# An S5 scan mixer with an MLP gate: even states in place of the direct matrix, row-half products, and a second product and outputs with features on partitions

## The chip, the core and the metric

The kernel runs on one core of a Trainium2 chip. The metric is device microseconds of one execution. The kernel before has a median of 153.38 us over three runs (153.37 to 153.44).

## What is computed

The input `x` has 2048 positions of 448 features, all tensors are bf16, and the weights are 448 by 448 or 448 by 1792 and back. Two branches read the normalised input, and their product is added to `x`.

```python
xn = layernorm(x)
# A: diagonal complex recurrence over the positions, 448 states
Bu = einsum("bld,pd->blp", xn, B_bar)
h  = Lam_bar * h + Bu[:, t, :]                  # t = 0 .. 2047
s  = 2 * einsum("blp,dp->bld", hseq, C).real + xn * Dskip
# B: MLP on a second layernorm
g  = silu(gelu(layernorm(xn) @ w1 + b1) @ w2 + b2)
out = x + s * g
```

## The kernel before

The 2048 positions are worked in four groups of 512. A group is two blocks of 256 positions, and on the chip 128 partitions hold a pair of neighbouring positions each, an even one and an odd one (`par` 0 and 1). The recurrence is run over pairs: one step of it takes the state over two positions, so a group has 256 steps (`NK`).

For each group the work is, by the names of the code:

- **Normalisation**: statistics on VectorE, scales on GpSimd or VectorE, two normalised copies (`xn_sb` for branch A, `xn2_sb` for B), each turned to features on partitions by transposing DMAs on SyncE's queue (`xnT`, `xn2T`).
- **First MLP product** (`mm1_run`, line 802): 14 blocks of 128 hidden features. The 448 input features are split into halves of 64 rows, so that two matmuls of 64 rows run beside each other on the two halves of TensorE's array. Blocks go in pairs through three pairs of PSUM banks; ScalarE's GELU (line 806) empties them into `gT`.
- **Second MLP product** (`mm2`, line 829): the 14 hidden blocks are the weights one by one, `w2` (448 columns) is what streams, and the result has positions on partitions. VectorE adds the bias (line 832). In groups 0 and 3 ScalarE then takes SiLU of it; in groups 1 and 2 it takes tanh, which needs no other function table than GELU's, and VectorE finishes the gate (line 837).
- **State inputs** (`bu`, line 730): `Bu` for a pair of positions needs 896 input features (an even and an odd position). Seven row blocks of states by seven chunks of 128 features give 49 matmuls of 256 columns a group. The matrix `BT` is `B` and `Lam*B` next to each other, formed in the kernel (`lb`, lines 659 to 662), and turned by transposing DMAs.
- **Recurrence** (`ssm`, lines 745 to 776): VectorE turns the inputs by a table of angles (`WT`), scans the decay (`TENSOR_TENSOR_SCAN`, line 754), ScalarE copies to bf16, VectorE turns back into `h_sb`. The tables come from ScalarE's Sin (line 641), which lies in SiLU's function table.
- **Outputs** (`ym`, lines 872 to 894): odd positions are `CQ` times the state; even positions are `CZ` times the state before, plus a direct matrix `M0` times the position's own input (line 875). `M0` is formed once by 28 matmuls (`m0`, lines 698 and 713). VectorE multiplies by the gate and adds `x`, SyncE stores.

TensorE starts with filler matmuls on constants (line 422).

Nothing of the order is decided on the chip. Every operation is a task, `ORDER` is a list of task numbers that sets the order of each engine, `SECOND` lists the tasks that run on the second of two permitted engines, and semaphore waits are put in from the tasks' reads and writes. Each engine takes its own instructions strictly in that order, so an instruction that waits holds up all behind it on that engine. The function tables of ScalarE are loaded by tasks as well; where a function is not in the table that is loaded, the build puts a load in.

## Time and profile before

| | |
|---|---|
| median of three runs | 153.38 us |
| profiled execution: span | 151.8 us |
| TensorE busy | 148.0 us, 98% |
| VectorE busy | 127.4 us, 84% |
| ScalarE busy | 99.0 us, 65% |
| GpSimd busy | 41.7 us, 27% |
| TensorE matmuls | 1135 |
| share of TensorE in the chain that ended last | 97% |

The profile's span runs from the first to the last instruction of one execution. The page gives no other time for that execution; the median of the timed runs is 1.6 us above the span, for what lies around it. The chain that ended last is followed back from the last instruction, at each step to what released it. It stands on TensorE nearly all the way, so what TensorE does, and when it waits, is the time.

### The profile page before, as it was taken

The page shows a single profiled execution, that of the slowest core. Times are in us where ns is not written, and L with a number is a line of the kernel's source. Part 1 is how long each engine was busy: PE and PEld are TensorE (multiplying, and loading weights), DVE is VectorE, ACT ScalarE, POOL GpSimd, SP SyncE. Part 2 cuts the span into 40 slices and gives each one's busy share as a digit, 9 for nine tenths or more (in the row PEclk, how much of TensorE's full clock was granted, in tenths as well). Part 3 has the DMA queues.
Part 4 walks back from the last instruction along what each step waited for, and adds up shares of the span by engine and source line. Part 5 has one row for each costly group of instructions (what it writes and reads, how often), then busy time and mean ns, then how long its engine had stood idle before and what let it go on. Part 6 is the DMA issues. An engine that isn't in the chain of part 4 may idle for free.

```text
span 151.8 us, 2990 instructions
## 1 busy us (share of the span) xinstructions
PE 148.0 (98%) x1135; PEld 87.9 (58%) x1135; DVE 127.4 (84%) x267; ACT 99.0 (65%) x183; POOL 41.7 (27%) x101
## 2 busy tenths in 40 slices
PE   7999999999999999999999999999999999999992
PEld 7986755454566577545444556764454666555551
DVE  2877979899969979999999996479968726999984
ACT  3797998878789549997898610463579834067410
POOL 5367872053020820010456006200072031000201
PEclk9999999999999999999999999999999999999999
DMA  4999999989896300700004032710331001100023
GB/s 113 251 308 393 274 235 147 180 157 131 150 271 175 68 0 0 138 0 4 0 0 63 4 60 41 158 60 5 60 97 26 4 0 52 69 0 0 4 78 103
DMA packets 31236, 14.73 MB, mean 97 GB/s; under 512 B 24752, under 2 KB 30774, under 8 KB 31222
## 3 DMA queue, kind: packets, MB, share of 16 engines
q1 hardware_dynamic: 30912, 14.26, 43.3%
q0 software_dynamic: 160, 0.23, 0.8%
q8 instruction: 9, 0.15, 0.4%
q14 instruction: 5, 0.04, 0.2%
q10 hardware_dynamic: 150, 0.05, 0.1%
HBM read 6.89 MB, written 1.84 MB: 57 GB/s over the span
## 4 chain that ended last, share of the span: by engine, by line
PE 97%; DVE 1%; issue 0%
PE psum L802 29%; PE psum L829 28%; PE psum L730 14%; PE psum L872 13%; PE psum L875 4%; PE psum L422 3%; PE psum L713 3%; PE psum L878 1%; PE psum L460 1%; PE psum L698 1%; DVE tmp L894 0%; DVE psum L888 0%; PE psum L603 0%; PE psum L530 0%; PE psum L531 0%
## 5 line engine op out<-in xcount | busy, mean ns | idle before, releaser
L802 PE MATMUL psum<-xn2T,w_sb 64*128 64x512 bf16 (+1 forms) x462 | 44.6, 345 | 0.1
L829 PE MATMUL psum<-w_sb,gT 128*128 128x448 bf16 x224 | 44.4, 353 | 0.0
L806 ACT ACTIVATE gT<-psum,b1f 128x512 bf16<-128x512 f32 (+1 forms) x66 | 36.0, 625 | 10.4 <-PE psum L802 10.2
L802 PEld LDWEIGHTS psum<-xn2T,w_sb 64*128 64x128 bf16 x462 | 23.9, 109 | 19.8 <-ACT gT L806 2.3
L829 PEld LDWEIGHTS psum<-w_sb,gT 128*128 128x128 bf16 x224 | 21.6, 98 | 20.3 <-issue 0.6
L417 ACT ACTIVATE u_sb<-psum 128x512 bf16<-128x512 f32 (+2 forms) x22 | 10.5, 478 | 23.0 <-PE psum L730 22.7
L730 PE MATMUL psum<-xnT,BT 128*128 128x256 bf16 x196 | 24.0, 273 | 0.0
L730 PEld LDWEIGHTS psum<-xnT,BT 128*128 128x128 bf16 x196 | 19.0, 98 | 5.4 <-issue 1.1
L894 POOL TENSOR_TENSOR tmp<-t,x_all 128x448 bf16<-128x448 bf16 x5 | 5.1, 1030 | 33.1 <-DVE t L891 30.7
L754 DVE TENSOR_TENSOR_SCAN s_w<-dk,vs 128x774 f32<-128x774 f32 x8 | 14.0, 1760 | 0.1
L501 ACT ACTIVATE xn_sb<-x_all,lnw 128x448 bf16<-128x448 bf16 (+2 forms) x21 | 13.0, 662 | 1.2 <-DVE xn_sb L500 1.1
L417 ACT ACTIVATE vs<-s_w 64x256 bf16<-64x256 f32 (+2 forms) x16 | 10.9, 681 | 2.6 <-DVE s_w L754 1.5
L872 PE MATMUL psum<-CZ,h_sb 128*128 128x448 bf16 x56 | 11.9, 353 | 0.0
L832 DVE TENSOR_TENSOR o<-psum,b2bc 128x448 f32<-128x448 f32 x16 | 9.8, 615 | 1.5 <-PE psum L829 1.3
L872 PE MATMUL psum<-CQ,h_sb 128*128 128x448 bf16 (+2 forms) x54 | 10.5, 332 | 0.0
L399 DVE BATCH_NORM_STATS2 lnst<-x_all 128x6 f32<-128x448 bf16 x12 | 7.0, 615 | 2.2 <-DMA x_all<-in_A_x_dram 2.2
L872 PEld LDWEIGHTS psum<-CZ,h_sb 128*128 128x128 bf16 x56 | 5.4, 98 | 4.7 <-DVE lnmv L405 0.4
L872 PEld LDWEIGHTS psum<-CQ,h_sb 128*128 128x128 bf16 x54 | 5.1, 98 | 4.0 <-DVE t L888 0.4
L875 PE MATMUL psum<-M,xnT 128*128 128x448 bf16 x32 | 7.4, 352 | 0.0
L886 DVE TENSOR_TENSOR Cr<-psum,xd 128x448 f32<-128x448 f32 x7 | 4.3, 621 | 3.5 <-PE psum L878 3.4
L481 POOL TENSOR_TENSOR lnw<-lnw,mhalf 128x8 f32<-128x8 f32 x3 | 7.1, 2367 | 0.2
L500 DVE TENSOR_SCALAR xn_sb<-x_all,lnw 128x448 bf16<-128x448 bf16 (+2 forms) x19 | 6.9, 397 | 0.0
(161 smaller groups left out, 191.3 us busy)
## 6 DMA issues: line engine op xcount, KB each, us to landing
out_dram<-tmp SPq DMA_DIRECT2D x7, 224.0 KB, 2.0
x_all<-in_A_x_dram SPq DMA_DIRECT2D x3, 448.0 KB, 4.2
w_sb<-in_B_w_dram SPq DMA_DIRECT2D x3, 448.0 KB, 8.5
w_sb<-in_B_w_dram SPq DMA_DIRECT2D x3, 384.0 KB, 4.8
vs<-in_A_C_re_dram SPq DMA_DIRECT2D x1, 392.0 KB, 11.3
Bn<-in_A_B_im_dram SPq DMA_DIRECT2D x1, 336.0 KB, 10.2
Bn<-in_A_B_re_dram SPq DMA_DIRECT2D x1, 336.0 KB, 10.6
vs<-in_A_C_im_dram SPq DMA_DIRECT2D x1, 336.0 KB, 11.1
```

The lines of the kernel that those rows point to most:

```text
L399: dve([lambda e, b=b, par=par, q=q: e.bn_stats(lnst[:, q, :], x_all[:, 2 * g + b, par, :])], [f"x{2 * g + b}"] , [f"st{q}"], 0.62, prio)
L417: kb.either(("act", [lambda e, o=o, i=i: e.activation(o, i, ACT.Copy) for o, i in pairs]), ("dve", [lambda e, o=o, i=i: e.tensor_copy(o, i ...
L481: power = fns + [lambda e: e.tensor_tensor(w(2), w(0), mhalf[:].to_broadcast([128, 2, nq]), ALU.pow), lambda e: e.tensor_tensor(w(3), mean ...
L501: ("act", [lambda e, o=o, i=i: e.activation(o, i, ACT.Identity, bias=nb, scale=rs) for o, i in parts], 0.75, 0.2)]
L730: fns = [lambda e, r=r, m=m, d=d: e.matmul(psum[:, 4, r * NK:(r + 1) * NK], BT[:, m, d, :], xnT[:, gx, d, :], start=(d == 0), stop=(d == 6 ...
L754: dve(lambda e, so=so, vi=vi: e.tensor_tensor_scan(so, dk[:].rearrange("p i c -> p (i c)"), vi, 0.0, ALU.mult, ALU.add), ["v", "vl", "dk", ...
L802: return lambda e: e.matmul(view(bk[k]), w1_sb[rows, d, fcol(2 * j + k)], rhs[rows, d, :, :], start=not second and n == 0, stop=second and ...
L806: act([lambda e, k=k: e.activation(gT[:, gb, 2 * j + k, :].rearrange("p (r c) -> p r c", r=2)[:, :, cols], view(bk[k]), ACT.Gelu_apprx_tan ...
L829: fns = [lambda e, fi=fi: e.matmul(psum[:, bk, 0:D], gT[:, gb, fi, q * 128:(q + 1) * 128], w2_sb[:, fi, :], start=(fi == 0), stop=(fi == N ...
L832: dve(lambda e: e.tensor_tensor(o2[:, fb, :], psum[:, bk, 0:D], b2bc[:], ALU.add), [f"ps{bk}", "b2bc"], [f"oo{fb}"], 0.62, prio - 76)
L872: fns = [lambda e, k=k: e.matmul(psum[:, bk, c0:c1], h_sb[:, hb, k, k0:k0 + 128], cm[:, k, c0:c1], start=(k == 0), stop=False) for k in ra ...
L875: fns += [lambda e, d=d: e.matmul(psum[:, bk, c0:c1], xnT[:, gx, d, xs], M0[:, d, c0:c1], start=False, stop=(d == 3)) for d in range(4)]
```

## The change

The kernel is rewritten in five respects. New names are those of the changed kernel.

1. **No direct matrix.** `M0` and its 28 matmuls go. The state inputs are now formed in two steps: first the part of the even positions (kept as `ue`), then the odd part is added in the same PSUM banks. VectorE adds `ue` to the turned state, and this even state `hz` gives the even outputs with `CQ`; the odd outputs take `CZ` times the state (`hx`).
2. **State inputs on row halves** (`bu_phase`): as in the first MLP product, 64 rows each, 98 matmuls of 256 columns a group, written as stages that stand between the phases of the next group's first MLP product. They take one of its three pairs of PSUM banks.
3. **Second MLP product with features on partitions** (`mm2`): `w2` is the weight, `gT` streams, 512 columns. Features 384 to 447 go as two column halves (64 columns wide, the two position parities beside each other). The bias is a column, so ScalarE takes **SiLU from PSUM** and VectorE's addition goes. SiLU is used in all four groups; ScalarE's table is switched to GELU and back in each.
4. **Outputs with features on partitions** (`yt`): 256 columns each, features 384 to 447 as column halves. The skip term is a VectorE operation from PSUM (groups 0 to 2) or a diagonal matrix `Dg` on TensorE (group 3). The product with the gate (`t3`) is turned back by transposing DMAs (`out_dma`, groups 0 to 2) or by TensorE (`out_pe`, group 3).
5. **The orders** `ORDER`, `SECOND` and `STEPS` are new. `mm2` and `yt` now take two PSUM banks in turn.

```diff
-                    fns = [lambda e, fi=fi: e.matmul(psum[:, bk, 0:D], gT[:, gb, fi, q * 128:(q + 1) * 128], w2_sb[:, fi, :],
-                                                     start=(fi == 0), stop=(fi == NF - 1)) for fi in range(a, z)]
...
-                dve(lambda e: e.tensor_tensor(o2[:, fb, :], psum[:, bk, 0:D], b2bc[:], ALU.add), [f"ps{bk}", "b2bc"], [f"oo{fb}"], 0.62, prio - 76)
...
+                        pe([lambda e, fi=fi: e.matmul(psum[:, bk, :], w2_sb[:, fi, 128 * j:128 * j + 128], gT[:, gb, fi, :], start=fi == 0, stop=fi == NF - 1)
+                            for fi in range(a, z)], rd, [f"ps{bk}"])
...
+                act(lambda e: e.activation(g_sb[:, gb, 512 * j:512 * j + n], psum[:, bk, 0:n], ACT.Silu, bias=b2c[:, j:j + 1]), [f"ps{bk}", "db", f"Ws{g}"], [f"g{gb}_{j}"])
...
+                            fns.append(lambda e, rows=rows, bank=bank, m=m, o=o, n=n: e.matmul(
+                                psum[:, bank, c * NK:(c + 1) * NK], BT[rows, m, 4 * o + n, :], xnT[rows, gx, 4 * o + n, :],
+                                start=not (odd or second or n or c), stop=bool(second and n == 3), skip_group_check=bool(odd or c)))
...
+                dve(lambda e: e.tensor_tensor(hz[:, hb, :, :], hx[:, hb, :, 0:NK], ue[:, hb, :, :], ALU.add),
...
+                    pe([lambda e, k=k: e.matmul(psum[:, bk, NK:512], CZ[:, k, cols], hx[:, hb, k, 1:NK + 1], start=k == 0, stop=k == 6) for k in range(7)], ko, [f"ps{bk}"])
+                    fns = [lambda e, k=k: e.matmul(psum[:, bk, 0:NK], CQ[:, k, cols], hz[:, hb, k, :], start=not by_pe and k == 0, stop=not by_pe and k == 6, skip_group_check=by_pe) for k in range(7)]
...
-                kb.add("act", lambda e: e.preload_act_table_set("gelu_apprx_tanh_and_others"), ["W"] * (g == 0) + [f"g{n % 8}" for n in range(4 * g, 4 * g + 4)] * (9 >> g & 1), [f"Wg{g + 1}"], sem=f"gelu{g + 1}")
...
+                    gelu_table(g, gate(g - 1))
```

The last pair of lines of the diff: the load of GELU's table for group 1 waited for the angle tables (`"W"`) as well as for the gate of group 0; now it waits for the gate alone.

How the instructions move is told at three places. The first is TensorE after the first MLP product of group 0. Before, with `gT,w_sb` the second MLP product (56 matmuls), `xn2T,w_sb` the first product of group 1 and `xnT,BT` the state inputs of group 0:

```order
L802 MATMUL psum<-xn2T,w_sb 128x2x128 x56
L829 MATMUL psum<-w_sb,gT 128x448 x56
L802 MATMUL psum<-xn2T,w_sb 128x512 x90
L730 MATMUL psum<-xnT,BT 128x256 x14
L802 MATMUL psum<-xn2T,w_sb 128x512 x8
```

After, with lines 785 and 788 the second MLP product, 663 the first and 692 the state inputs:

```order
L663 MATMUL psum<-xn2T,w_sb 128x2x128 x56
L785 MATMUL psum<-gT,w_sb 128x512 x42
L788 MATMUL psum<-gT,w_sb 64x256 x28
L692 MATMUL psum<-xnT,BT 128x256 x28
L663 MATMUL psum<-xn2T,w_sb 128x512 x28
L692 MATMUL psum<-xnT,BT 128x256 x12
L663 MATMUL psum<-xn2T,w_sb 128x512 x6
```

The state inputs moved from behind the first product of group 1 to its front and between its phases. The last row is the third pair of hidden blocks, which goes into the banks of the first pair and so needs the first two GELUs of group 1 done.

The second place is ScalarE between the gate of group 0 and the GELUs of group 1. Before (line 834 is SiLU, 641 Sin, 619 the load of GELU's table):

```order
L834 ACTIVATE g_sb<-o 128x448 x2
L641 ACTIVATE WT<-s_w,sgn 128x256
L834 ACTIVATE g_sb<-o 128x448
L619 ACT_TABLE_LOAD
L806 ACTIVATE gT<-psum,b1f 128x512 x12
```

After (line 791 is SiLU, 590 Sin, 451 and 457 the normalised input, 605 a product with a coefficient of `B`, 476 the load that the code asks for):

```order
L605 ACTIVATE tmp<-Bn,cw 128x512
L451 ACTIVATE xn_sb<-x_all,lnw 128x448
L590 ACTIVATE WT<-s_w 128x3x258
L590 ACTIVATE WT<-s_w,sgn 128x4x258
L457 ACTIVATE xn_sb<-xn_sb 128x2x64
L791 ACTIVATE g_sb<-psum,db 128x256
L791 ACTIVATE g_sb<-psum,db 128x512
L590 ACTIVATE WT<-s_w,sgn 128x258
L476 ACT_TABLE_LOAD
L590 ACT_TABLE_LOAD
L590 ACTIVATE WT<-s_w,sgn 128x258
L669 ACT_TABLE_LOAD
```

The last Sin now stands behind the load of GELU's table. It is not in that table, so the build puts a load ahead of it and another behind it.

The third place is the end of VectorE's list. Before (line 888 is the product with the gate, 894 the addition of `x`):

```order
L888 SCALAR_TENSOR_TENSOR t<-psum,g_sb 128x448
L888 SCALAR_TENSOR_TENSOR t<-psum,g_sb 128x256
L894 TENSOR_TENSOR tmp<-t,x_all 128x448
L888 SCALAR_TENSOR_TENSOR psum<-psum,g_sb 128x192
L894 TENSOR_TENSOR tmp<-psum,Cr 128x192
```

After (line 826 is the skip term, 828 the product with the gate, 770 the even states of group 3, 843 and 862 additions of `x`, 862 from TensorE's transposes):

```order
L770 TENSOR_TENSOR Bn<-hx,ue 128x1792
L826 SCALAR_TENSOR_TENSOR tmp<-xnT,db,psum 128x512
L828 TENSOR_TENSOR t<-tmp,g_sb 128x512 x2
L828 TENSOR_TENSOR t<-psum,g_sb 128x512
L862 TENSOR_TENSOR Bn<-psum,x_all 128x4x128
L828 TENSOR_TENSOR t<-psum,g_sb 128x512
L843 TENSOR_TENSOR Bn<-Cr,x_all 128x2x384
L828 TENSOR_TENSOR t<-psum,g_sb 128x512
L843 TENSOR_TENSOR Bn<-Cr,x_all 128x2x384
L862 TENSOR_TENSOR Bn<-psum,x_all 128x4x128 x2
L828 TENSOR_TENSOR t<-psum,g_sb 128x256
L862 TENSOR_TENSOR Bn<-psum,x_all 128x4x64
```

The state chain of group 3, the outputs of group 2 and those of group 3 now end on VectorE in one list, and behind the last product TensorE turns it back before the last addition.

More of the change, by code (lines that the diff above doesn't have):

```diff
@@ L11 @@
 F32 = dt.float32
-PINNED = -1e5
 ENGS = ("pe", "act", "dve", "pool", "sp")
@@ new lines, in one_mm @@
+                def one_mm(k, n, h):
+                    rows, d = slice(64 * h, 64 * h + 64), (0, 1, 2 + h, 3 - h)[n]
+                    return lambda e: e.matmul(view(bk[k]), w1_sb[rows, d, fcol(2 * j + k)], rhs[rows, d, :, :], start=not second and n == 0, stop=second and n == 3)
+                pe([one_mm(h if not second else 1 - h, n, h) for n in range(4 if second else 3) for h in (0, 1)],
+                   xk2 + [f"w1_{c}", f"w1r_{c}"] + ([f"w1c_{c}"] if second else []), [f"ps{bk[0]}", f"ps{bk[1]}"], split=True)
```

962 lines of the change are left out of this document (459 added, 503 removed), and 36 rows, old and new, of the table ORDER.

## The prediction

> **What bounds the kernel now.** I read the page first, then the chain that ended last, then ScalarE's and VectorE's timelines around the places where TensorE will newly have to wait.
>
> ```profile
> span 151.8 us, 2990 instructions
> PE 148.0 (98%) x1135; PEld 87.9 (58%) x1135; DVE 127.4 (84%) x267; ACT 99.0 (65%) x183; POOL 41.7 (27%) x101
> PE 97%; DVE 1%; issue 0%
> ```
>
> TensorE is busy from end to end and is the chain. Work taken off it is worth its full length, and any wait that the new order puts on it costs its full length, since it has no idle time left to absorb one. VectorE at 84% is the next.
>
> The chain in order of time gives the pace of each kind of matmul (start, length, line, count):
>
> ```profile
> 5.14 0.43 PE psum L460 x4
> 7.36 2.44 PE psum L802 x42
> 9.79 0.55 PE psum L460 x8
> 19.53 10.70 PE psum L829 x56
> 30.23 10.04 PE psum L802 x90
> 53.45 1.53 PE psum L730 x14
> 54.98 1.32 PE psum L713 x7
> 64.09 0.87 PE psum L698 x7
> 84.95 1.32 PE psum L872 x7
> 86.28 0.76 PE psum L875 x4
> 89.68 1.14 PE psum L872 x6
> 90.82 0.19 PE psum L878
> 148.32 0.12 PE psum L878
> ```
>
> So 448 columns take 0.191 us (10.70 / 56), which makes 512 columns 0.218; 256 columns on full rows 0.109 (1.53 / 14); 256 columns on half rows 0.058 (2.44 / 42) and 512 on half rows 0.112 (10.04 / 90). The seven matmuls of line 698 are column halves: 0.87 us, where seven full ones take 1.32 (line 713) and four would take 0.76. So column halves run beside each other too, and I take 0.058 for one of 256 columns.
>
> **The change part by part: TensorE's work.** The direct matrix goes: 3 x 1.32 + 0.87 = 4.83 us. The outputs of a group were two times (1.32 + 0.76) and two times (1.14 + 0.19), 6.82; they become 42 matmuls of 256 columns and 14 column halves, 42 x 0.109 + 14 x 0.058 = 5.40. Over four groups that is 5.7 less. Group 3 adds the skip term on TensorE (three of 512 columns, two halves) and 14 transposes at 0.069 (0.55 / 8): 0.65 + 0.12 + 0.97 = 1.74 more. The state inputs go from 196 x 0.109 to 392 x 0.058: 1.3 more. The second product goes from 224 x 0.191 = 42.8 to 168 x 0.218 + 112 x 0.058 = 43.1: 0.3 more. The sum is -4.83 - 5.7 + 1.74 + 1.3 + 0.3 = **-7.2 us**. If the column halves did not overlap, 168 of them would cost 0.051 more each, 8.6 us; the row of line 698 is the nearest and speaks against it.
>
> **The start.**
>
> ```profile
> 4.00 1.14 PE L422 MATMUL psum<-const-bfloat16-1.0 128*128 128x128 bf16 x9
> 6.62 0.30 PE L603 MATMUL psum<-ident,dk 4*128 4x3 bf16 x4
> 7.00 0.17 DVE L606 COPY b1f<-psum 128x14 f32<-128x14 f32 x1 [0.58 <-PE psum L604]
> L417 DVE COPY xn2T<-psum 128x512 bf16<-128x512 bf16 x2 | 0.8, 420 | 0.0
> ```
>
> The fillers are as many as before, but 21 instead of 13 now stand ahead of the second pair of transposes; 8 x 0.12 is 1.0 later, and its copy (0.42) must follow, so the first MLP product starts some 0.6 late. The bias columns that the first GELU needs (ready at 7.17) now stand on VectorE behind six others and come near 9.7; 0.4 more. Five small matmuls for the new bias and skip columns: 0.3. **+1.3**, between 0.3 and 2.
>
> **The function table of group 1.**
>
> ```profile
> 25.18 1.72 ACT L641 ACTIVATE WT<-s_w 128x768 bf16<-128x768 f32 x2 [0.49 <-DVE s_w L632]
> 26.93 1.69 ACT L641 ACTIVATE WT<-s_w,sgn 128x1024 bf16<-128x1024 f32 x2
> 29.46 0.49 ACT L641 ACTIVATE WT<-s_w,sgn 128x256 bf16<-128x256 f32 x1
> 31.00 0.58 ACT L834 ACTIVATE g_sb<-o 128x448 bf16<-128x448 f32 x1 [1.05 <-DVE o L832]
> 31.65 1.28 ACT L619 ACT_TABLE_LOAD   x1
> 33.03 3.58 ACT L806 ACTIVATE gT<-psum,b1f 128x512 bf16<-128x512 f32 x6
> L501 ACT ACTIVATE xn_sb<-x_all,lnw 128x448 bf16<-128x448 bf16 x9 | 6.6, 758 | 0.1
> L659 ACT ACTIVATE tmp<-Bn,cw 128x448 f32<-128x448 bf16 x1 | 0.7, 654 | 0.0
> ```
>
> Before, the first GELU of group 1 ran at 33.03, 2.8 us behind the start of its matmuls at 30.23, and TensorE went on in two other pairs of banks. After, ScalarE has behind the second SiLU (about 27.3 by the same durations, when VectorE has the angles ready too) three large Sins (0.86, 0.86, 1.2), two normalisations (0.76 each), a product (0.74), a copy (0.3), two SiLUs (0.4, 0.65), Sin (0.49), then load, load, Sin, load: 3 x 1.28 + 0.49. Pipelined by 0.08 each that is 10.6, so the first GELU is near 37.9 and the first pair of banks free at 39.2. TensorE: the second product starts near 20.5 and takes 42 x 0.218 + 28 x 0.058 = 10.8; 28 state inputs (1.6), 28 of the first product (3.1) and 12 state inputs (0.7) bring it to 36.8, where the third pair of blocks needs those banks. It waits **2.4 us**; none if the angles come 2.5 us sooner, 4.4 if they come 2 later. Queued behind that wait are all state inputs of group 0, and VectorE waits for them.
>
> The Trainium skill (ScalarE: Activation LUTs, "What ACT_TABLE_LOAD costs") puts a switch at about 2.66 us with its drain. Here load and first use are 1.38 apart (31.65 to 33.03), and I use that; by the page the two extra loads would add 2.6 us, and the time would be 158.5.
>
> The state inputs themselves move to 31.3:
>
> ```profile
> 32.90 6.26 SPq L83 DMA_TRANSPOSE BT<-Bn  x4
> BT<-Bn SPq DMA_TRANSPOSE x7, 3.9
> xnT<-xn_sb SPq DMA_TRANSPOSE x8, 3.0
> ```
>
> Before, the first `BT` was sent at 32.90. Now the loads of `B` stand ahead of `w2` on SyncE's queue and the products on VectorE's list ahead of most angle work, so I count the fourth `BT` sent near 25.5 and landed near 29.5. I cost it at nothing; the cover is 1.8 us. The transposed input of group 1's first product lands at about 33, just when it is needed.
>
> **Later waits.** In group 0 VectorE finishes `CQ` some 0.4 us after TensorE wants it: **+0.4**. The first product now has two bank pairs instead of three. Where no state inputs stand between its phases (42 matmuls in a row in group 2), a pair is refilled only 1.2 (two GELUs) + 0.2 after its end, with 8 x 0.112 = 0.9 of work between: twice 0.6, and 0.2 twice ahead of it: **+1.6**, between 0.5 and 2.5. In group 1 the outputs take the bank of the product just ended:
>
> ```profile
> L834 ACT ACTIVATE g_sb<-o 128x448 bf16<-128x448 f32 x8 | 4.3, 570 | 3.3 <-DVE o L832 3.1
> L886 DVE TENSOR_TENSOR Cr<-psum,xd 128x448 f32<-128x448 f32 x7 | 4.3, 621 | 3.5 <-PE psum L878 3.4
> ```
>
> SiLU of 512 columns (0.65) plus 0.15 to start, twice, and once the skip term (0.70 + 0.15): **+2.4**, between 0.8 and 3. In group 3 a state-input stage waits **0.3** for a copy.
>
> **The state chain.**
>
> ```profile
> L754 DVE TENSOR_TENSOR_SCAN s_w<-dk,vs 128x774 f32<-128x774 f32 x8 | 14.0, 1760 | 0.1
> L774 DVE TENSOR_TENSOR h_sb<-pa,pb 128x1536 bf16<-128x1536 bf16 x4 | 3.8, 958 | 0.1
> L417 ACT ACTIVATE vs<-s_w 128x1536 bf16<-128x1536 f32 x4 | 5.9, 1487 | 1.6 <-DVE s_w L754 1.5
> ```
>
> Six wide operations (5.7), small ones (1.4), scans of 786 and 1048 elements (1.8 + 2.4), the copy (1.5) and the new even states (1792 elements, 1.1) are 13.9 us a group; with what VectorE's list puts between, 16.6 in group 3. From state inputs done near 126 that ends at 143, when TensorE has just finished the outputs of group 2: no wait, and no margin. I count margins of -0.4, 2, 1.2 and 0 us in the four groups.
>
> **The end.**
>
> ```profile
> 149.50 0.36 DVE L894 TENSOR_TENSOR tmp<-psum,Cr 128x192 bf16<-128x192 f32 x1
> 149.89 0.38 ACTq L84 DMA_DIRECT2D out_dram<-tmp  x1
> ```
>
> Now the last product ends at 148.44, and 3.35 follow, 1.9 of them from the last store's issue. After, behind it come on VectorE two additions of 512 columns (0.6 each), a product (0.35), two transposes (0.3 with their start), an addition (0.35), gaps (0.6), then the 1.9: 4.7. **+1.35**, between -0.5 (its queue empty by then) and 3 (additions of group 2 waiting ahead for their transposes, 3.0 us from issue).
>
> **The sum**: -7.2 + 1.3 + 2.4 + 0.4 + 1.6 + 2.4 + 0.3 + 1.35 = +2.55 us on the span of 151.8. The median of the runs is 1.6 above the span, 153.38, so 155.9 (+1.7%). What a measurement of this kernel tells from no change is about 0.2%, 0.3 us.
>
> **The rivals.**
>
> ```profile
> PEclk9999999999999999999999999999999999999999
> L832 DVE TENSOR_TENSOR o<-psum,b2bc 128x448 f32<-128x448 f32 x16 | 9.8, 615 | 1.5 <-PE psum L829 1.3
> ```
>
> *Faster, VectorE early.* It loses 16 bias additions, 8 gate products and the products of the direct matrix. If its list then runs some 2 us ahead of my count, the angles are early (the table wait falls to 0.4), `CQ`, the copy and the last additions are in time: -7.2 + 1.3 + 0.4 + 1.6 + 2.4 = -1.5, 151.9. For it: 9.8 us of bias additions alone come off VectorE. Against it: skip, gate and wider copies come back, and the chain now has the even states. It decides where the angles are ready before 25. With the bank waits also covered it reaches 150.
>
> *Slower, the state chain.* If it is 2 us longer than counted, the margins turn into 2 + 0 + 0.8 + 2 more: 160.7. It decides at the first even product of each group.
>
> *Slower, `BT` late.* If the transposes go out only 6 us earlier than the first of before (32.90, four in 6.26), TensorE stands 4 us at 31.3: 160.
>
> *The halves do not overlap*, and the change is not what it says: 392 x 0.051 + 8.6 = 29 us, 184. Lines 802 and 698 speak against it.
>
> *A slow stretch after a wait.* Transposes of one form took 0.107 each at 5.14 and 0.069 at 9.79, while the page's row of the granted clock (PEclk) stays in its highest tenth; should a wait at 37 us bring the early pace back for 3 us, the price is about 1.5: 157.4. The Trainium skill (TensorE: Matmul & The Clock Gate, "Part 1: The HAM clock gate") says that an idle window of about 3.4 us halves the clock until a busy one has passed. No stretch of before has such an idle time.
>
> **How the numbers follow.** My forecast has a chance of 0.48, VectorE early 0.32, the long state chain 0.10, `BT` late 0.04, the slow stretch 0.03, no overlap 0.03. Of VectorE early some 0.03 falls within 0.2% of no change, as does 0.02 of the forecast. So faster 0.29, same 0.05, slower 0.66. The range takes in the faster rival with its lower reach and the long chain: 150.0 to 161.0. The forecast's own range, from its terms' bounds, is 153.3 to 159.
>
> **What would show it.** Right: TensorE's group of direct-matrix matmuls gone and its busy time near 141; an idle time of 1 to 4 us on TensorE near 37 us put down to ScalarE's GELU behind three loads in a row; short waits on SiLU in the outputs of group 1; a tail over 4 us from the last product. Wrong: no wait near 37, or waits at `BT`; the column halves at 0.1 us each; a total of idle time on TensorE under 4 us (then it is faster) or over 12.

## The result, and the profile after

The changed kernel takes 159.33 us (median of four runs, 157.67 to 159.45), the kernel before 153.41 beside it. The ratio is 1.035, with an interval of 1.030 to 1.040. The forecast was 155.9, slower, with a range up to 161.0: the direction was right, the loss of 5.9 us more than twice the 2.5 of the forecast. The profiled execution took 159.38 us with a span of 157.6, so 1.8 lie around it.

The page of the kernel after: its span, its busy times, and the chain that ended last.

```profile
span 157.6 us, 3653 instructions
PE 144.3 (92%) x1450; PEld 93.9 (60%) x1456; DVE 133.5 (85%) x270; ACT 100.2 (64%) x179; POOL 46.0 (29%) x101
PE 39%; DVE 22%; ACT 17%; DMA 12%; issue 3%; POOL 3%; SPq 2%; ACTq 0%; DVEq 0%; POOLq 0%
```

TensorE's busy time fell by 3.7 us, its idle time rose from 3.8 to 13.3, and the chain, 97% TensorE before, now passes through four kinds of work. TensorE's timeline after (start, length, line; in brackets the wait just before and what ended it) shows where:

```profile
8.72 2.33 PE L663 MATMUL psum<-xn2T,w_sb 64*128 64x256 bf16 x20 [0.43 <-DVE w_sb L307]
...
23.34 9.01 PE L785 MATMUL psum<-gT,w_sb 128*128 128x512 bf16 x41 [0.16 <-DVE tmp L606]
32.28 1.72 PE L788 MATMUL psum<-gT,w_sb 128*64 128x256 bf16 x28
33.93 1.94 PE L692 MATMUL psum<-xnT,BT 64*128 64x256 bf16 x28
36.53 3.20 PE L663 MATMUL psum<-xn2T,w_sb 64*128 64x512 bf16 x28 [0.66 <-DMA xn2T<-xn_sb]
...
41.93 0.84 PE L663 MATMUL psum<-xn2T,w_sb 64*128 64x512 bf16 x6 [1.54 <-ACT gT L669]
...
46.04 1.94 PE L692 MATMUL psum<-xnT,BT 64*128 64x256 bf16 x28 [0.89 <-DMA BT<-Bn]
...
51.91 0.83 PE L692 MATMUL psum<-xnT,BT 64*128 64x256 bf16 x12 [0.55 <-DMA xnT<-xn_sb]
...
70.72 0.94 PE L806 MATMUL psum<-Bn,CQ 128*128 128x256 bf16 x7
...
153.69 0.29 PE L856 MATMUL psum<-ident,t 128*128 128x128 bf16 x2 [0.95 <-DVE t L828]
```

The second product began at 23.34, where the forecast had 20.5. The first product's first 20 matmuls of 64 rows took 2.33 us, 0.116 each, twice as long as in the kernel before (0.058). The granted clock reads 1.00 from 8.72 to 11.06 us; it does not show this slow pace. Behind the start there are three short waits for transposing transfers (0.66, 0.89, 0.55), which the forecast put at nothing, and one of 1.54 for a GELU. The cause of that one stands on ScalarE, whose timeline there reads:

```profile
36.19 1.28 ACT L476 ACT_TABLE_LOAD   x1
37.49 1.28 ACT L590 ACT_TABLE_LOAD   x1
38.78 0.51 ACT L590 ACTIVATE WT<-s_w,sgn 128x258 bf16<-128x258 f32 x1
39.31 1.28 ACT L669 ACT_TABLE_LOAD   x1
40.61 2.42 ACT L669 ACTIVATE gT<-psum,b1f 128x512 bf16<-128x512 f32 x4
```

Three loads, each about 1.3 us to the next instruction, with one Sin between them: the table wait that was forecast (near 37 us, 2.4). It came at 40.4 to 41.9, since all that precedes it was late.

SyncE's queue, on which all transposing transfers stand (a row's length is the time in which the queue took them in; x2 is two of them):

```profile
16.55 5.62 SPq L77 DMA_TRANSPOSE xnT<-xn_sb  x1
...
25.60 4.04 SPq L77 DMA_TRANSPOSE BT<-Bn  x3
...
31.04 1.31 SPq L77 DMA_TRANSPOSE xn2T<-xn_sb  x1
32.40 0.59 SPq L78 DMA_DIRECT2D Bn<-in_A_B_im_dram  x1
33.03 1.31 SPq L77 DMA_TRANSPOSE xn2T<-xn_sb  x1
34.39 1.29 SPq L77 DMA_TRANSPOSE Cr<-vs  x1
...
36.36 1.23 SPq L77 DMA_TRANSPOSE BT<-Bn  x1
...
41.40 2.69 SPq L77 DMA_TRANSPOSE BT<-Bn  x2
44.14 0.58 SPq L78 DMA_DIRECT2D x_all<-in_A_x_dram  x1
44.76 3.49 SPq L77 DMA_TRANSPOSE xnT<-xn_sb  x2
```

One transpose holds the queue for 1.2 us or more (1.23 for the `BT` at 36.36), and the first of them, which stands behind the loads of the start, for 5.62. Between 16.55 and 48.25 the queue is never free for more than 0.2 us. The kernel before asks for the same set-up of group 0, but its state inputs stand at 40.21 and its first output at 77.53. After, they stand at 33.93 and 69.66: the change asks for the same transposes 6 to 8 us sooner.

After the first even product (70.72), TensorE waits only 0.95, 0.17, 0.46 and 0.95 us to the end, and the rest of the program, 86.9 us here, is as long within 0.1 us in the profile of every variant of the changed kernel below.

### The profile page after: what moved, and what is told of

Its sections match the earlier page's. It is cut to its first block, busy times and chain, and to the rows that moved or that the text cites. A ratio compares the mean times of both kernels' runs of the same rounds, so it can differ in the third digit from the quotient of the medians.

```text
span 157.6 us, 3653 instructions
## 1 busy us (share of the span) xinstructions
PE 144.3 (92%) x1450; PEld 93.9 (60%) x1456; DVE 133.5 (85%) x270; ACT 100.2 (64%) x179; POOL 46.0 (29%) x101
## 4 chain that ended last, share of the span: by engine, by line
PE 39%; DVE 22%; ACT 17%; DMA 12%; issue 3%; POOL 3%; SPq 2%; ACTq 0%; DVEq 0%; POOLq 0%
PE psum L785 11%; PE psum L663 11%; PE psum L692 5%; ACT gT L669 5%; ACT tmp L605 4%; DMA xnT<-xn_sb 4%; PE psum L806 4%; DMA Cr<-vs 3%; DVE s_w L751 3%; PE psum L805 2%; DVE t L828 2%; ACT vs L306 2%; PE psum L788 2%; DMA x_all<-in_A_x_dram 2%; DVE vs L307 2%
## 5 line engine op out<-in xcount | busy, mean ns | idle before, releaser
L669 ACT ACTIVATE gT<-psum,b1f 128x512 bf16<-128x512 f32 (+1 forms) x66 | 37.1, 625 | 9.1 <-PE psum L663 7.1
L785 PE MATMUL psum<-gT,w_sb 128*128 128x512 bf16 x162 | 36.2, 379 | 0.9 <-issue 0.7
L692 PE MATMUL psum<-xnT,BT 64*128 64x256 bf16 x392 | 26.2, 269 | 3.0 <-DMA xnT<-xn_sb 1.5
L785 PEld LDWEIGHTS psum<-gT,w_sb 128*128 128x128 bf16 x168 | 16.0, 98 | 19.6 <-issue 0.8
L692 PEld LDWEIGHTS psum<-xnT,BT 64*128 64x128 bf16 x392 | 18.9, 94 | 11.7 <-issue 3.6
L791 ACT ACTIVATE g_sb<-psum,db 128x512 bf16<-128x512 f32 (+1 forms) x16 | 10.0, 631 | 17.6 <-PE psum L785 11.9
L751 DVE TENSOR_TENSOR_SCAN s_w<-vs,dk 128x786 f32<-128x786 bf16 (+1 forms) x8 | 18.0, 2261 | 0.0
L826 DVE SCALAR_TENSOR_TENSOR tmp<-xnT,db,psum 128x512 f32<-128x512 bf16 (+1 forms) x15 | 9.6, 637 | 2.7 <-PE psum L806 2.3
L806 PE MATMUL psum<-Bn,CQ 128*128 128x256 bf16 x84 | 11.1, 272 | 0.3 <-DVE Bn L770 0.2
L805 PE MATMUL psum<-hx,CZ 128*128 128x256 bf16 x84 | 11.3, 273 | 0.0
L451 ACT ACTIVATE xn_sb<-x_all,lnw 128x384 bf16<-128x384 bf16 (+2 forms) x17 | 10.2, 639 | 0.0
```

The costliest lines, as they stand in the source:

```text
L451: ("act", [lambda e, o=o, i=i: e.activation(o, i, ACT.Identity, bias=nb, scale=rs) for o, i in parts]),
L669: act(lambda e, k=k, fi=fi: e.activation(gT[:, gb, fi, :].rearrange("p (r c) -> p r c", r=2)[:, :, cols], view(bk[k]), ACT.Gelu_apprx_tanh ...
L692: fns.append(lambda e, rows=rows, bank=bank, m=m, o=o, n=n: e.matmul(psum[:, bank, c * NK:(c + 1) * NK], BT[rows, m, 4 * o + n, :], xnT[ro ...
L751: dve(lambda e, so=so, vi=vi, di=di: e.tensor_tensor_scan(so, vi, di, 0.0, ALU.add, ALU.mult), ["v", "vl", "vz", "dk", "dk01"] + ["v3"] * ...
L785: pe([lambda e, fi=fi: e.matmul(psum[:, bk, :], w2_sb[:, fi, 128 * j:128 * j + 128], gT[:, gb, fi, :], start=fi == 0, stop=fi == NF - 1) f ...
L791: act(lambda e: e.activation(g_sb[:, gb, 512 * j:512 * j + n], psum[:, bk, 0:n], ACT.Silu, bias=b2c[:, j:j + 1]), [f"ps{bk}", "db", f"Ws{g ...
```

## The experiments

The theory from this profile: the slow start (2.8 us) makes the loss, since waits behind it are short. The rival: the set-up of group 0 is held by transfers and their users, and what TensorE gains ahead of them turns into waits. All runs are compared with the kernel before on the same chip; "first even" is the start of the first row of line 806 (810 in e8) in the one execution of each that was profiled. Runs of one kernel differ by up to 3.6 us (e17: 156.90 to 160.50), so a difference of some tenths in that column alone shows nothing.

| run | median us | ratio to before, 95% interval | first even, us |
|---|---|---|---|
| after | 159.33 | 1.035 (1.030 to 1.040) | 70.72 |
| e1 | 159.13 | 1.036 (1.031 to 1.041) | 70.41 |
| e2 | 160.22 | 1.046 (1.040 to 1.051) | 71.19 |
| e4 | 159.78 | 1.043 (1.038 to 1.048) | 70.69 |
| e5 | 158.76 | 1.032 (1.026 to 1.038) | 70.21 |
| e6 | 161.65 | 1.053 (1.046 to 1.060) | 72.76 |
| e7 | 160.92 | 1.048 (1.042 to 1.054) | 71.99 |
| e8 | 158.27 | 1.033 (1.029 to 1.036) | 69.77 |
| e9 | 158.85 | 1.035 (1.033 to 1.037) | 70.40 |
| e10 | 158.66 | 1.035 (1.030 to 1.040) | 71.28 |
| e11 | 162.17 | 1.055 (1.050 to 1.060) | 74.08 |
| e12 | 158.31 | 1.032 (1.026 to 1.037) | 68.80 |
| e13 | 159.15 | 1.037 (1.032 to 1.041) | 70.30 |
| e14 | 158.94 | 1.037 (1.033 to 1.040) | 69.85 |
| e15 | 159.69 | 1.036 (1.030 to 1.042) | 71.02 |
| e16 | 159.00 | 1.034 (1.029 to 1.039) | 70.38 |
| e17 | 157.77 | 1.029 (1.022 to 1.035) | 68.36 |
| e18 | 158.16 | 1.033 (1.029 to 1.037) | 69.72 |

**The start: e1, e2, e3, e4.** e1 adds fillers in the gaps of the start:

```diff
-            dummies(4, ["st0"])
+            dummies(9, ["st0"])
...
-                    + [... ident[32:36, 35:36], ...) for k in range(2)],
+                    + [... ident[32:36, 35:36], ...) for k in range(2)] + [lambda e: e.matmul(psum[:, 4, 128:256], one, one, start=True, stop=True)] * 4,
```

> The changed kernel with nine matmuls on constants more on TensorE: five ahead of the first transposes (idle 0.55 us at 5.57) and four behind the bias columns (idle 0.43 at 8.29). All else is the same. Theory 'slow pace' (the idle moments at the start keep TensorE at half its pace until 13 us): the first 20 matmuls of line 663 take 0.058 each and not 0.116, and the time falls by 1.3 to 2.3 us from 159.4, to 157.1 to 158.1. Rival 'VectorE order' (the late normalisation alone makes the start late): no gain, 159.3 to 159.7, since the additions only fill idle time.

e2 moves a statistic (99) behind a normalisation (106) on VectorE:

```diff
-... 105 97 99 95 106 2 ...
+... 105 97 95 106 99 2 ...
```

> The changed kernel with one instruction moved on VectorE: the first statistics of block 1 behind the first normalisation of block 0, so the transposes come at 5.5 and not 6.1 and TensorE has no idle time ahead of them. Theory 'slow pace': the first transposes 0.6 earlier and the full pace from about 7 us, 1.5 to 2.5 us less, 156.9 to 157.9. Rival 'VectorE order' without any change of pace: 0.6 less at most, 158.8. Third theory (ScalarE's GELU bounds the first 23 us anyway): within 0.3 of 159.4.

e3 is the kernel before with eight fillers fewer:

```diff
-dummies(9, ["vr0"])
+dummies(5, ["vr0"])
...
-dummies(5, ["xm0p0"], 1)
+dummies(1, ["xm0p0"], 1)
```

> The kernel before with eight matmuls on constants fewer (four ahead of the first transposes, four ahead of the first product), so that TensorE stands idle for about 0.4 us twice, as in the changed kernel. No other work changes, and the fillers' results are not used. Theory 'slow pace': the first product's matmuls take 0.116 each until about 13 us, 1.5 to 2.3 us more, 154.9 to 155.7. Rival (no effect of so short an idle time): 153.1 to 153.6, the same as before or a little less.

e4 puts the last Sin (202) ahead of the load of GELU's table (303), so that one load is left of three:

```diff
-... 357 303 310 202 321 ...
+... 357 202 303 310 321 ...
```

> The changed kernel with the last Sin ahead of GELU's table load on ScalarE, which leaves one load instead of three near 37 us. Theory 'on the path': the wait of 1.54 us for GELU at 41.93 goes and the time falls by 1.2 to 1.6, to 157.8 to 158.2. Rival 'given back': the third pair starts 1.5 earlier, but the later waits for transfers (BT at 46.04, the transposed input at 51.91) grow by as much, 159.0 to 159.6.

e1 has the full pace from the first product on (20 matmuls in 1.30 us) and starts the second product at 21.08, 2.3 us sooner. Its end hardly moves (span 157.3 against 157.6). TensorE's rows of e1 say where the 2.3 us went:

```profile
36.40 3.20 PE L663 MATMUL psum<-xn2T,w_sb 64*128 64x512 bf16 x28 [2.79 <-DMA xn2T<-xn_sb]
...
45.67 1.94 PE L692 MATMUL psum<-xnT,BT 64*128 64x256 bf16 x28 [2.35 <-DMA BT<-Bn]
...
51.61 0.83 PE L692 MATMUL psum<-xnT,BT 64*128 64x256 bf16 x12 [0.62 <-DMA xnT<-xn_sb]
```

The first product of group 1 begins at 36.40 instead of 36.53, and the next waited transfers at 45.67 and 51.61 instead of 46.04 and 51.91. The waits for transfers are 5.8 us where the kernel after shows 2.1: they took in the 2.3 of the start and the 1.5 of the GELU wait, which is gone. The theory of the start fell. e4's profiled execution had the full pace without any filler (second product at 20.59, as forecast), and lost the GELU wait too:

```profile
35.92 4.89 PE L663 MATMUL psum<-xn2T,w_sb 64*128 64x512 bf16 x28 [2.79 <-DMA xn2T<-xn_sb]
...
46.03 1.94 PE L692 MATMUL psum<-xnT,BT 64*128 64x256 bf16 x28 [1.52 <-DMA BT<-Bn]
...
51.88 0.83 PE L692 MATMUL psum<-xnT,BT 64*128 64x256 bf16 x12 [0.54 <-DMA xnT<-xn_sb]
```

The state inputs of group 1 start at 51.88, where they did. Two terms of the forecast, start and tables, are real but bring nothing when they are taken away. The 28 matmuls behind the wait took 4.89 us, where they take 3.20 in the kernel after: a slow stretch that costs 1.7. The granted clock shows this one: it reads 0.50 between 37.60 and 39.30 us of e4. e2 (second product at 20.70) shows the same, with waits of 1.15 for `BT` and 3.55 for `xn2T` and 28 in 4.89, and is slower.

e3 is 1.003 times the kernel before (1.000 to 1.006, ten runs, median 153.77), and its profiled execution (153.25) has the full pace. But three of its ten runs took 154.65 to 155.00, about what the theory of the slow pace expected, where the 13 runs of the kernel before took 153.65 at most, and none of the three has a trace. So fewer fillers do not bring the slow start in each run; whether they bring it in some is not shown. Up to 30 us e4's lists are those of the kernel after, and yet its start has the full pace: the start differs from one execution to the next. In the kernel after VectorE waited for a load of `x` till 5.14 us, in e1 and e4 it went on at 4.49. The cause of the slow start is not settled.

**The transfers: e5 to e10.** Built on e1. e5 moves a small load (36, the second of a pair with 34) to the front and the load of blocks 6 and 7 (240) behind a transpose (287):

```diff
-... 208 34 295 ... 222 36 313 ... 311 240 312 ... 256 287 436 ...
+... 208 34 36 295 ... 222 313 ... 311 312 ... 256 287 240 436 ...
```

> The kernel of e1_fillers (159.1) with two loads moved on SyncE's queue: the 64-row imaginary part of B (56 KB) from between the two transposes of group 1's first product to behind the other 64-row part, and the load of blocks 6 and 7 behind the transposes of group 1's state inputs. Theory 'SyncE's queue' (from 16 to 48 us it sends one transfer after another, 1.3 us each, and TensorE waits for the late ones at 36.4, 45.7 and 51.6): the waits fall by one or two slots of 0.6, and the time by 0.6 to 1.5, to 157.6 to 158.5. Rival 'ScalarE and VectorE' (their work between 36 and 52 sets the pace, the transfers are only the last in it): 158.9 to 159.3.

It is the fastest so far by its median, but the intervals overlap. `BT` is waited for 0.38 us only (46.10); the wait for `xn2T` is 3.02 and brings the slow stretch (28 in 4.89).

e6 is e5 with the queue reordered for its users, the last three `BT` sooner and the `Cr` later, and the loads of `x` without their wait for a transpose. The lines of names are SyncE's issues behind the fourth `BT`, as `ORDER` now gives them:

```diff
-ldx(4, 2, ["Ct0"]) ... ldx(6, 2, ["Ct0"])
+ldx(4, 2) ... ldx(6, 2)
...
-Cr xn2T Bn xn2T Cr x BT Cr Cr BT BT x xnT xnT
+xn2T BT xn2T BT Cr Cr BT x Cr Cr xnT xnT x
```

> The kernel of e5 with SyncE's queue in the order in which TensorE needs the transfers: the transposes BT of B (2, 5 and 6) and of group 1's first product ahead of most transposes of C, the load of blocks 4 and 5 no longer tied to the first of these, blocks 6 and 7 last. Theory 'SyncE's queue': the waits for BT (2.35 at 45.67 in e1) and for the state inputs of group 1 (0.62) go, that for the first product shrinks by 0.6, and the time falls by 2 to 3.5 against 159.1, to 155.6 to 157.1. Rival 'ScalarE and VectorE': the waits move to GELU and the outputs of group 0 start no earlier than 68.9, 158.6 to 159.3. Third (C comes late instead, VectorE's CZ waits): 159.5 to 161.

e7 is e6 with e4's Sin:

> The kernel of e6 with the last Sin ahead of GELU's table load. If the transfers were what covered the two extra loads in e4, then with the queue in order the loads are on the path: 1 to 2 us less than e6. If ScalarE has time left there: within 0.3 of e6.

Both are slower than e5; e7's median is 0.7 below e6's, with intervals that overlap. In e6 the wait for `BT` is gone, and others stand in its place, one each on ScalarE, VectorE and TensorE:

```profile
45.34 0.67 ACT L605 ACTIVATE tmp<-Cr,cw 128x448 f32<-128x448 bf16 x1 [4.13 <-DMA Cr<-vs]
```

```profile
43.59 1.15 DVE L377 BATCH_NORM_STATS2 lnst<-x_all 128x6 f32<-128x448 bf16 x2 [8.07 <-DMA x_all<-in_A_x_dram]
```

```profile
47.12 2.26 PE L692 MATMUL psum<-xnT,BT 64*128 64x256 bf16 x28 [3.79 <-ACT u_sb L306]
```

ScalarE stands at a product with `C`, and behind it on its list stands the copy `u_sb` that TensorE needs. A queue that is served in another order moves the wait to the list that was written for the old one.

e8 leaves out the load of blocks 4 and 5 but for four elements (group 2 is computed from blocks 2 and 3), e9 puts that load (239) ahead of the small ones, e10 is e9 with e4's Sin:

```diff
-            ldx(4, 2)
+            ld("sp", x_all[0:1, 4:6, 0, 0:2], dram_ap(A_x, 4 * 256 * D, [[2 * D, 1], [256 * D, 2], [1, 2]]), ["x4", "x5"])
```

> The kernel of e5_small_load_early (158.8) without the load of blocks 4 and 5 (448 KB at 36.4 us, 4.2 us to landing): group 2 is computed from blocks 2 and 3 again. No other work changes. Theory 'C late' (VectorE's long stretch from the products with C to the even states of group 0 begins when the last transpose of C and blocks 4 and 5 have landed, and the first even product follows 27 to 29 us behind: 43.6 and 70.7 in the changed kernel, 45.3 and 72.8 in e6): the transposes of C land 2 to 3 us earlier, the first even product starts near 67.7 and the time falls by 1.8 to 3, to 155.8 to 157. Rival 'TensorE's own waits' (only its waits for transfers at 36 to 52 count): 0.4 to 0.8 less, 158 to 158.4.

> The kernel of e5 with the load of blocks 4 and 5 earlier on SyncE's queue, ahead of the loads of C, and so out of the transposes. Theory 'C late': VectorE takes the statistics of blocks 4 and 5 in its idle time at 35 to 41 us, the transposes of C come 0.5 to 1.5 us earlier since the load is moved and not gone, and the time falls by 0.5 to 1.8, to 157 to 158.3. Rival 'the rate of the transfers decides alone' (all of them are only shifted): 158.5 to 159.2.

> The kernel of e9 with the last Sin ahead of GELU's table load. If VectorE's stretch behind C decides, ScalarE's two loads are covered: within 0.4 of e9. If ScalarE has become the last, 1 to 2 us less.

In e8 VectorE's first product with `C` came 0.9 us sooner than in e5 (42.57 against 43.47), and the first even product 0.4 us. That is not enough to make the landing of `C` alone the cause. e9 and e10 changed the waits (`BT` 1.44 and `xn2T` 3.01; 0.54 and 3.33) and not the end.

**The lists of all three engines: e11, e13.** e11 orders SyncE's, ScalarE's and VectorE's lists together, with the loads of `C` behind `xn2T`. e13 mends a step of e11 on which ScalarE waited for VectorE, and puts the last `BT` ahead of the transposes of `C`. SyncE's issues behind the fourth `BT`, in the kernel after, in e11 and in e13:

```diff
-Cr xn2T Bn xn2T Cr x BT Cr Cr BT BT x xnT xnT
+xn2T xn2T C C C BT BT x Cr Cr BT Cr Cr xnT xnT x
+xn2T xn2T C C C BT BT BT x Cr Cr Cr Cr xnT xnT x
```

> The kernel of e5 with three lists changed together, TensorE's left as it is. SyncE: the loads of C behind the transposes of group 1's first product, then BT, blocks 4 and 5, the transposes of C. ScalarE: the last Sin ahead of the table load; the copies and GELUs that free TensorE's banks ahead of the products with C. VectorE: the same copies and the first two products of the state inputs ahead of most products with C. Theory 'three things are late together' (the first product's input at 36.5, C at 43.5, then VectorE's full stretch to the first even product at 70.2 to 71.2, so that taking one away gains little): now all give way, the first product of group 1 starts near 33.5, the first even product at 67 to 68.7, and the time falls by 1.5 to 3 against 158.8, to 155.8 to 157.3. Rival 'C's landing alone sets it': C's loads are later and land no sooner, 158.5 to 160.

> The kernel of e11 with its three lists set right where e11 stood still: ScalarE's GELUs ahead of the product with C that waits for VectorE, and the last BT ahead of the transposes of C. Theory 'transfers up to 52' (in every run so far 105.7 us lie between the state inputs of group 1 on TensorE, 51.9 in the changed kernel, and the end, whatever was changed on VectorE; only TensorE's waits ahead of that count): these state inputs start at 46 to 48.7, and the time is that start plus 107.4 if VectorE keeps up, 153.5 to 156.1. Rival 'VectorE's stretch' (C's landing near 44 to 46, then 25 us of work to the first even product): the first even product stays at 69.5 to 71 with a wait ahead of it, time 157.5 to 159.

In e11 the first product of group 1 had no wait (33.42), but TensorE stood 2.36 us for `BT`, ScalarE 2.92 us for VectorE, and TensorE 3.82 us till 53.35, with a slow stretch behind it. In e13 all waits for set-up transfers are gone from TensorE's timeline up to the first even product, and it reaches the stage that begins at 50.39 in e5 at 45.73, 4.7 us sooner. It loses them again at once:

```profile
44.72 1.18 PE L692 MATMUL psum<-xnT,BT 64*128 64x256 bf16 x14 [0.60 <-DVE u_sb L715]
...
48.82 0.83 PE L692 MATMUL psum<-xnT,BT 64*128 64x256 bf16 x12 [2.06 <-ACT gT L669]
...
54.81 0.83 PE L692 MATMUL psum<-xnT,BT 64*128 64x256 bf16 x12 [2.13 <-ACT ue L306]
```

The GELU that ended the second of these waits stood on ScalarE behind a product with `C`, and that one had waited:

```profile
46.08 0.67 ACT L605 ACTIVATE tmp<-Cr,cw 128x448 f32<-128x448 bf16 x1 [2.83 <-DMA Cr<-vs]
```

So with the transfers mended, the landing of `C` comes back through ScalarE's strict list.

**What stands behind `C`: e12, e14 to e18.** Two suspects were left: ScalarE's list, and VectorE's work between the landing of `C` and the first even product. In e12 (on e5) and e14 (on e13) the scans of group 0 are plain copies, so that group's recurrence is left out:

```diff
-... e.tensor_tensor_scan(so, vi, di, 0.0, ALU.add, ALU.mult) ...
+... e.tensor_copy(so, vi) if g == 0 else e.tensor_tensor_scan(so, vi, di, 0.0, ALU.add, ALU.mult) ...
```

> The kernel of e5 in which VectorE copies in place of the two scans of group 0 (1.8 and 2.3 us; the recurrence of that group is left out, no operand changes its size). Theory 'VectorE's stretch' (from 43.6 to the first even product VectorE is busy but for 2 us and sets the time): about 2 us less there, first even product at 67.9 to 68.7, time 156.2 to 157.2. Rival 'TensorE and ScalarE need as long anyway': the first even product moves by under 0.7, time over 158.

> The kernel of e13 with copies in place of the two scans of group 0 (the recurrence of that group is left out), 2.9 us less on VectorE. Theory 'transfers up to 52': the same as e13, within 0.5, as in e12 against e5. Rival 'VectorE's stretch': 1.5 to 2.9 less than e13. If e13 shows a wait ahead of the first even product, this run tells how much of it is VectorE's.

The scans' 1.79 + 2.33 us became 0.56 + 0.69. In e12 the first even product came 1.4 us sooner than in e5; but its wait for `xn2T` was 2.35 and brought no slow stretch (28 in 3.20), and that alone is 1.7. In e14 the same cut brought 0.45. So VectorE's scans hold it by some tenths at the most.

e15 mends ScalarE's list of e13 once more: in group 0, a GELU (323) and a copy (349) ahead of the products with `C`, two copies (442, 441) ahead of the normalisations of group 2; four steps of VectorE for the same state inputs move forward too. e16 is e15 with the copies for scans.

> e13 with ScalarE's list mended once more: in group 0 the GELU and the copy of the third pair stand ahead of the first product with C, and the two copies of the early state inputs stand ahead of the normalisations of group 2, so that on ScalarE only the steps that need C still wait for it. Theory (what is left of set-up behind the landing of C near 45 us is VectorE's, some 24 us of work of which 1.65 us stood idle in e13): the waits of TensorE at 48.8 and 54.8 go, 3 to 4 us of them, but the first even product comes no earlier than 69.3 us and the time stays at 158 to 159 us. Rival (ScalarE's list alone held it): the first even product at 67 to 68 us, time 155.5 to 157 us.

> e15 with plain copies in place of the scans of group 0 (the recurrence of that group is left out), which takes some 2.9 us of work off VectorE behind the landing of C. Theory (VectorE's stretch): first even product at 67 to 68 us, time 156 to 157.2 us, 2 to 3 us ahead of e15. Rival (ScalarE's list alone): e16 and e15 within 0.5 us of one another, both at 155.5 to 157 us. If both stay at 158 to 159 us, neither of the two is what holds the first even product.

Both theories missed. The first even product of e16 is 0.6 us ahead of e15's and its median 0.7, where the theory had 2 to 3; and both stay at 159 and more, where the rival had 157 at most. TensorE now waited for another transfer, the last `xnT` (2.77 us in e15, till 48.59), and 1.7 us for GELUs at 58.4 and 61.1; behind the first of these waits the pace was slow again (granted clock 0.55 from 48.60 to 52.40). The table of busy times by stretch has in e15, between 50 and 70 us (columns: the stretch, then length and busy time of PE, weight loads, VectorE, ScalarE and GpSimd):

```profile
50.00:70.00 20.00, 18.30 (x149) 10.07 (x146) 18.13 (x31) 17.70 (x29) 0.54 (x2) 0.94 0.24 27
```

and in the kernel before and the kernel after, in this order:

```profile
50.00:70.00 20.00, 20.00 (x142) 12.20 (x141) 18.91 (x34) 16.05 (x33) 4.46 (x8) 1.00 0.19 36
```

```profile
50.00:70.00 20.00, 19.13 (x178) 11.22 (x176) 18.49 (x30) 18.87 (x33) 0.00 (x0) 1.00 0.14 27
```

In the kernel after ScalarE has 18.87 us of work where it had 16.05, and GpSimd none where it had 4.46. TensorE, VectorE and ScalarE are each over 92% full there, and each takes its list in strict order.

e17 takes work off ScalarE in the main (the scaled copies of `C` over 64 of 448 columns, the few of VectorE too), e18, which has the copies for scans as well, off both:

```diff
-                n = o.shape[-1]
+                n = o.shape[-1]; h = 64 if n == 448 else n
...
-... e.activation(tmp[o, k, 0:n], b[i], ACT.Copy, scale=c[i]) ...
+... e.activation(tmp[o, k, 0:h], b[i][:, 0:h], ACT.Copy, scale=c[i]) ...
```

> e15 in which the scaled copies of C (the first of the two operations of each product with C, 0.67 us on ScalarE, 0.44 on VectorE) are made over 64 of their 448 columns, so that the rest of each product is computed from stale data. That takes some 3.8 us of work off ScalarE between the landing of C and the first even product, and under 1 us off VectorE. Theory (between 50 and 70 us ScalarE and VectorE are both full, 17.7 and 18.1 of 20 us in e15, so that lightening one alone shows the other): e17 gains at most 1 us on e15, as e16 did. Rival (ScalarE's work alone holds it): the first even product at 67.4 us, 18.8 behind the transfer at 48.6, and a time of 156 to 157 us.

> e17 with the plain copies of e16 in place of the scans of group 0: both engines are lightened, ScalarE by some 3.8 us and VectorE by 2.9 or more. Theory (both full): the first even product at 67.4 to 68 us, where the last awaited transfer (48.2 to 48.6) and TensorE's own work of 18.8 us put it, and a time of 156 to 157 us. Rival (neither engine's amount of work, but the order of the lists): within 0.7 us of e16, at 158.3 or more.

TensorE's rows of e17 and of e18 where the last awaited transfers come, and at the GELUs of group 1 behind them:

```profile
48.53 0.83 PE L692 MATMUL psum<-xnT,BT 64*128 64x256 bf16 x12 [2.65 <-ACT tmp L605]
...
56.38 1.47 PE L785 MATMUL psum<-gT,w_sb 128*128 128x512 bf16 x6 [0.19 <-ACT gT L669]
58.40 3.63 PE L785 MATMUL psum<-gT,w_sb 128*128 128x512 bf16 x16 [0.55 <-ACT gT L669]
```

```profile
48.91 1.46 PE L692 MATMUL psum<-xnT,BT 64*128 64x256 bf16 x12 [3.01 <-DMA xnT<-xn_sb]
50.14 1.51 PE L663 MATMUL psum<-xn2T,w_sb 64*128 64x512 bf16 x6
```

e17 has the lowest median of all variants, its first even product 2.7 us sooner than e15's: 1.0 of it are the GELU waits (0.51 + 1.19 became 0.19 + 0.55), and 1.8 the slow stretch behind 48.6, which is not in this run (12, 6 and 16 matmuls in 0.83, 0.83 and 1.05, where e15 has 1.27, 1.52 and 1.72). The profile names a product on ScalarE (`tmp`) as the end of e17's wait at 48.53; these matmuls do not read it, and the second `xnT`, sent at 45.2, took at least 3.2 us to land, so I put the wait down to that transfer. The intervals of e15 and e17 overlap, so the gain is likely and not shown. e18, lighter by VectorE's scans too, is no faster: it had the slow stretch again (12 in 1.46, then 6 in 1.51). The theory that both engines together hold it fell; ScalarE's work holds about 1 us in these profiles, and the rest is the transfer that lands near 48.5 and the pace behind the wait for it.

## Why the prediction was right in sign and wrong in size

**The failed step** is the sentence "I cost it at nothing; the cover is 1.8 us. The transposed input of group 1's first product lands at about 33, just when it is needed." It followed the first four `BT`, and these were in time (no wait at 33.93, nor at 31.67 in e1); it gave the last three no place on the queue, though the state inputs at 46 need them, and they were sent from 36.36 on. It let `xn2T` land at 33, and the product that needs it began between 35.9 and 37.1 in after, e1, e4 and e5. It has no word on the `xnT` of group 1. With a start as forecast, the waits for these three transfers, costed at nothing, are 5.8 us in e1 and 4.9 plus a slow stretch of 1.7 in e4. The rival "`BT` late", with a chance of 0.04, came near: TensorE stands for transposes. But it put 4 us at 31.3, on transfers that were in time there, where the waits are at three later places.

**The balance** is best drawn on e1, whose start is near the forecast's. The table by stretch of e1 for TensorE alone (length and busy time first):

```profile
0.00:24.00 24.00, 21.61 (x270) 1.00 1.01 251
24.00:50.00 26.00, 20.67 (x219) 1.00 1.05 188
50.00:71.00 21.00, 19.95 (x183) 1.00 0.15 29
71.00:120.00 49.00, 47.42 (x504) 1.00 0.32 57
120.00:157.30 37.30, 31.96 (x298) 1.00 0.19 57
sum 157.30, PE 141.63; mean PE 28.33
```

TensorE is busy 141.6 us, where the forecast gives 140.8 (148.0 - 7.2), and idle 15.7, where it gives 13.5 (3.8 of before and the 9.75 of its waits). Of the idle time the transfers are 5.8, costed at nothing. The table wait (2.4) does not appear here; in the kernel after it is 1.54. The waits for `CQ`, the banks and the copy, 4.7 together, are 2.8 with all small gaps. The tail is 0.5 more than forecast, the start 0.1. That is +0.8 + 5.8 - 2.4 - 1.9 + 0.5 + 0.1 = +2.9, from the 154.35 of the forecast to e1's span of 157.3. So two terms that were too large hide 4.3 of the 5.8. With them as e1 has them the forecast's +2.55 would have been -1.75, faster: that its sign came out right is luck. In the kernel after itself the second product begins 2.8 later than forecast (2.5 by the forecast's own +1.3, which behind 19.53 makes 20.8 and not 20.5), and the transfers are waited for 2.1 only: there the start looks like the cause, and e1 and e4 show that its loss comes back as waits for transfers when it is taken away.

**Right**: TensorE's work. The column halves overlap (28 of line 788 in 1.65 us from start to start, 0.059 each), the direct matrix is gone, and the -7.2 us of work are -6.4 in e1, with its nine more fillers. Three loads stand in a row on ScalarE, and TensorE waits 1.54 for the GELU behind them (1 to 4 expected). The tail is 5.2 us from the last product (152.4 to 157.6) against 4.7. Of its signs of being wrong two came: "waits at `BT`", and an idle time over 12 us (13.3). And one sign of being right did not: in the outputs of group 1 there is no wait on SiLU, and the only one put down to another engine, 0.17 us, is for VectorE's even states; the forecast had 2.4 us for this place. TensorE's busy time, forecast near 141, is 144.3 in the kernel after, with the slow start, and 141.6 in e1.

**The table switch.** The sum by the trace, 1.38 from a load to the first use, held: 36.19 to 37.49 and 39.31 to 40.61 are 1.30 each. By the 2.66 of the Trainium skill (ScalarE: Activation LUTs, "What ACT_TABLE_LOAD costs") the GELU behind three loads would have come an estimated 4 us later; this case's traces show 1.30, and the measurement decides.

**The slow stretch** was a rival with a chance of 0.03 and a price of 1.5: it occurs, costs 1.7 in e2, e4 and e5, and does not occur in the profile of the kernel after, whose longest wait is 1.54. The granted clock reads 0.50 in it (37.60 to 39.30 us of e4). The Trainium skill (TensorE: Matmul & The Clock Gate, "Part 1: The HAM clock gate") has the clock halved after an idle window of some 3.4 us, and the window free-running. The second part fits: waits of 2.79 brought the stretch in e4 and not in e1. The first is too long as a limit here, since 2.57 us of waiting brought it in e16.

**VectorE early, the state chain, the bank waits.** None decided. From the state inputs at 51 to 52 us to the first even product it is 18.8 us in after, e1, e2, e4 and e5, the same for each start, and 18.8 in e12 with copies for scans: TensorE's own work (busy 17.6 of the last 18.0 us in e1), not VectorE's chain.

**What stays open.** The waits for transfers are measured, but no run shows that they alone make the loss: e13 took them off TensorE up to the first even product, and waits for GELUs and copies on the same set-up came in their place. No run gained the 5.8 us back; e17 comes nearest, and its gain is not clear of the noise. Open, too, is how near the rewrite can come to the kernel before. With the last awaited transfer at 48.2 to 48.9 as in e15, e16 and e18, 18.8 behind it and 86.9 to the end, the span would be 153.9 to 154.6, an estimate, and the time about 156: still slower. An order that has this transfer sooner was not found in these runs. Why the start was slow in the kernel after and in full pace in e4 is open as well.

## What to carry to other kernels

A kernel whose TensorE is full hides its set-up; a change that takes TensorE work off the front, or moves users of the set-up forward, asks for the same transfers sooner, and each of them must be costed with its place on the queue and its landing, the second and third of a name as well as the first. A wait that looks like the cause in one profile may only be the first of several that end at nearly the same time: take it away, and see whether the stage behind the next transfer moves. Where engines serve strict lists, a transfer moved up or down must be followed through every list that was written around its landing.

## What was not expected of the hardware

- TensorE's pace at the start differs between executions that read the same clock (1.00): 0.116 a matmul in the kernel after, 0.065 in e1 (20 in 1.30), and the same 0.065 in e4 without added fillers.
- Behind waits of 2.57 us (e16) to 3.82 us (e11) the pace is halved for a few us in some profiles, with a granted clock of 0.50 (37.60 to 39.30 us of e4), and not in others (2.79 in e1, 2.89 in e6, 2.65 in e17).
- A transposing transfer holds SyncE's queue 1.2 us at the least, and 5.62 for the first one, behind the loads of the start, in the kernel after.
